# First batch's squares summed on VectorE, wider unread products and a later sigmoid table in a cross-covariance attention and gated feed-forward kernel

## The chip, the cores and the metric

One core of one Trainium2 chip. The metric is the device time of one launch in microseconds; medians of several launches are given with their range. The runs were spread over four chips, each round with runs of the kernel before of its own. A profile is one more execution with the hardware profiler, and its span (first to last recorded instruction) is some 2 us shorter than the time of the launch.

## The reference, cut to what matters

```
B, N, C = 4, 6016, 256                       # q, k, v; d_ff = 1536
qn = q / (norm(q over N) + 1e-6);  kn likewise
s  = kn^T @ qn / tau                          # C x C per batch
a  = softmax(s)
x  = (v @ a) as 24064 x 256
out = (sigmoid(x @ w_gate) * (x @ w_val)) @ w_out
```

Per batch, everything up to `a` is a reduction over N. So the first batch's q and k have to be in before any token of its output can start; the later batches' reductions run beside the feed-forward of the batch before.

## The kernel before

q and k of batch 0 come in 13 groups: eleven of four 128-row tiles (numbered 0 to 10), one of two tiles, one of one. Per group VectorE squares q, ScalarE squares k, TensorE adds to the scores, and the column sums of the squares are one-column products with a vector of ones. Between these stand products that nobody reads, there to keep the array's clock up (without those of groups 0 to 8, in run b0 below, group 10's scores took 1.87 us instead of 1.03).

```
def norm_mms(ps, sqs, nt, first, last, order=(0, 1)):
    for w in order:
        for u in range(nt):
            for j in range(CB):               # 2 per tile and operand: 16 per group
                mm(ps[:, one column], sq[:, u, 128 columns], ones_bf[:, 0:1], ...)

def busy(n):                                  # unread products, 128 wide
    for _ in range(n):
        mm(ps[:, :P], ones_bf, ones_bf, True, True)

busy(40)
for g, (t0, nt) in enumerate(groups0):
    sq = [squares(q of group) on VectorE, squares(k of group) on ScalarE]
    for u in range(nt): score(0, t0, u)       # 8 products of 256 columns per group
    ...
    if full: busy(6)
    norm_mms(ps_n0, sq, nt, g == 0, g == last0, ...)
    if full and not the last full one: busy(6)
# norms -> ps_rk -> x -> exp -> e, then the products of e with the expert weights:
sums(0, 0)
gh(0, 0, psg, "g", act=False)                 # act: which engine evicts it
gh(0, 1, psv, "v", act=True)
nc.scalar.preload_act_table(ACT.Sigmoid)
sums(0, 1, pss, "s")
gh(0, 2, psg, "g", act=False)
gh(0, 3, psv, "v", act=False)
gh(0, 4, pso, "o", act=True)
# ... (cut) the steady loop: glu(f): gate and val products, sigmoid, multiply;
# in its first seven steps also gh(0, 5 + f, pso, "o")
```

Products 0 to 4 of e with the weights, their evictions (gh_G, gh_H) and the load of the sigmoid table are a serial passage ahead of the loop.

## Time and profile before

| | before |
|---|---|
| median of 6 runs | 832.36 us (832.06 to 832.71) |
| span of the profile | 830.4 us |
| group 10's scores begin (the loads are in) | 32.33 us |
| from there to the first ps_rk product | 3.47 us |
| from ps_rk to the first ps_o product | 20.09 us |
| from the first ps_o to the end | 774.5 us |

These four rows cut the span at TensorE's own events, and they add up to it. The first is set by the loads, the next two are the serial passage and the first loop steps, the last is steady work that the change does not touch. The profile lines are in the prediction.

### The profile page before, as it was taken

The page shows a single profiled execution, that of the slowest core. Times are in us where ns is not written, and L with a number is a line of the kernel's source. Part 1 is how long each engine was busy: PE and PEld are TensorE (multiplying, and loading weights), DVE is VectorE, ACT ScalarE, POOL GpSimd, SP SyncE. Part 2 cuts the span into 40 slices and gives each one's busy share as a digit, 9 for nine tenths or more (in the row PEclk, how much of TensorE's full clock was granted, in tenths as well). Part 3 has the DMA queues.
Part 4 walks back from the last instruction along what each step waited for, and adds up shares of the span by engine and source line. Part 5 has one row for each costly group of instructions (what it writes and reads, how often), then busy time and mean ns, then how long its engine had stood idle before and what let it go on. Part 6 is the DMA issues. An engine that isn't in the chain of part 4 may idle for free.

```text
span 830.4 us, 14273 instructions
## 1 busy us (share of the span) xinstructions
PE 818.9 (99%) x5463; PEld 513.8 (62%) x5474; DVE 570.4 (69%) x981; ACT 390.8 (47%) x642; POOL 82.9 (10%) x159
## 2 busy tenths in 40 slices
PE   8899999999999999999999999999999999999998
PEld 7656666666666666665576666666566566666666
DVE  2477777777667777777767777777766666666664
ACT  4554444445644444444654444444555444444442
POOL 5532100002110100000220020000000000000000
PEclk9999999999999999999999999999999999999999
DMA  9999623236755543233974453223222324323211
GB/s 209 207 206 189 130 52 88 51 63 123 141 105 105 102 105 60 56 52 79 161 140 97 84 112 77 51 75 66 62 56 65 75 51 82 71 49 69 47 36 71
DMA packets 78740, 77.21 MB, mean 93 GB/s; under 512 B 50768, under 2 KB 55632, under 8 KB 78672
## 3 DMA queue, kind: packets, MB, share of 16 engines
q0 software_dynamic: 23920, 38.81, 28.2%
q1 hardware_dynamic: 54608, 36.97, 17.4%
q8 instruction: 43, 0.70, 0.3%
q10 hardware_dynamic: 144, 0.52, 0.2%
q14 instruction: 25, 0.20, 0.1%
HBM read 78.64 MB, written 24.64 MB: 124 GB/s over the span
## 4 chain that ended last, share of the span: by engine, by line
PE 95%; DMA 3%; DVE 1%; issue 0%; POOL 0%; ACT 0%; POOLq 0%; DVEq 0%; ACTq 0%
PE ps_o L88 30%; PE ps_gate L88 29%; PE ps_val L88 29%; PE ps_s L88 4%; DMA k_sb<-in_k_dram 3%; PE ps_gh L88 2%; PE ps_n L88 0%; DVE gh_G L363 0%; PE ps_busy L88 0%; POOL q_sb L97 0%; PE ps_r L88 0%; DVE hT L408 0%; PE ps_rk L88 0%; DVE gh_H L363 0%; DVE x_sb L293 0%
## 5 line engine op out<-in xcount | busy, mean ns | idle before, releaser
L408 DVE TENSOR_TENSOR hT<-ps_val,g_sb 128x512 bf16<-128x512 f32 (+1 forms) x576 | 391.4, 680 | 214.7 <-ACT g_sb L407 209.5
L407 ACT ACTIVATE g_sb<-ps_gate 128x512 bf16<-128x512 f32 (+1 forms) x576 | 338.2, 588 | 386.6 <-PE ps_gate L88 379.0
L88 PE MATMUL ps_gate<-vT,gh_G 128*128 128x512 bf16 (+1 forms) x1152 | 337.6, 375 | 0.6 <-ACT g_sb L407 0.4
L88 PE MATMUL ps_val<-vT,gh_H 128*128 128x512 bf16 (+1 forms) x1152 | 337.7, 375 | 0.2
L88 PE MATMUL ps_o<-w_out_sb,hT 128*128 128x256 bf16 x2256 | 326.2, 273 | 0.0
L88 PEld LDWEIGHTS <-hT 128*128 128x128 bf16 x2256 | 220.7, 98 | 124.7
L88 PEld LDWEIGHTS <-gh_H 128*128 128x128 bf16 x1152 | 112.7, 98 | 131.5 <-DVE gh_H L363 0.5
L88 PEld LDWEIGHTS <-gh_G 128*128 128x128 bf16 x1152 | 112.5, 98 | 37.9 <-issue 0.6
L106 POOL DMA_DIRECT2D v_sb<-in_v_dram x48 | 25.6, 533 | 625.6 <-DMA vT<-v_sb 517.4
L434 DVE COPY out_sb<-ps_o 128x256 f32<-128x256 f32 x188 | 77.8, 414 | 13.5 <-PE ps_o L88 13.5
L88 PE MATMUL ps_s<-k_sb,q_sb 128*128 128x256 bf16 x376 | 66.8, 275 | 4.9 <-DMA k_sb<-in_k_dram 3.2
L212 DVE TENSOR_TENSOR acc<-acc,sq 128x1024 bf16<-128x1024 bf16 (+1 forms) x66 | 44.2, 670 | 0.0
L88 PEld LDWEIGHTS <-q_sb 128*128 128x128 bf16 x376 | 36.8, 98 | 11.1 <-issue 4.5
L173 DVE TENSOR_TENSOR sq<-q_sb 128x1024 bf16<-128x1024 bf16 (+2 forms) x45 | 30.0, 669 | 18.5 <-DMA q_sb<-in_q_dram 10.7
L97 POOL DMA_DIRECT2D q_sb<-in_q_dram x48 | 26.3, 548 | 15.6 <-DMA q_sb<-in_q_dram 7.9
L97 POOL DMA_DIRECT2D k_sb<-in_k_dram x48 | 26.4, 550 | 12.0 <-ACT g_sb L407 5.4
L173 DVE TENSOR_TENSOR sq<-k_sb 128x1024 bf16<-128x1024 bf16 (+2 forms) x34 | 22.4, 658 | 1.1 <-PE ps_n L88 1.1
L361 ACT ACTIVATE gh_G<-ps_gh,rrow 128x512 bf16<-128x512 f32 x22 | 15.1, 687 | 12.9 <-PE ps_gh L88 9.1
L171 ACT ACTIVATE sq<-k_sb 128x1024 bf16<-128x1024 bf16 (+1 forms) x12 | 12.1, 1020 | 14.7 <-DMA k_sb<-in_k_dram 13.2
L363 DVE TENSOR_SCALAR gh_H<-ps_gh,rrow 128x512 bf16<-128x512 f32 x23 | 17.1, 743 | 1.6 <-PE ps_gh L88 1.6
L88 PE MATMUL ps_busy<-ones_bf 128*128 128x128 bf16 x182 | 16.6, 244 | 1.1 <-DVE shift L125 1.1
L88 PEld LDWEIGHTS <-ones_bf 128*128 128x128 bf16 x194 | 14.6, 110 | 1.5 <-DVE shift L125 1.1
(54 smaller groups left out, 112.6 us busy)
## 6 DMA issues: line engine op xcount, KB each, us to landing
out_dram<-out_sb SPq DMA_DIRECT2D x44, 512.0 KB, 2.9
v_sb<-in_v_dram POOLq DMA_DIRECT2D x44, 256.0 KB, 3.9
q_sb<-in_q_dram POOLq DMA_DIRECT2D x43, 256.0 KB, 7.1
k_sb<-in_k_dram POOLq DMA_DIRECT2D x43, 256.0 KB, 8.3
out_dram<-out_sb SPq DMA_DIRECT2D x4, 384.0 KB, 2.5
w_gate<-in_moe_w_gate_dram POOLq DMA_DIRECT2D x3, 256.0 KB, 6.8
w_val<-in_moe_w_val_dram POOLq DMA_DIRECT2D x3, 256.0 KB, 6.8
w_out_sb<-in_moe_w_out_dram POOLq DMA_DIRECT2D x1, 768.0 KB, 11.9
```

Of the source, the lines that this page charges most:

```text
L88: nc.tensor.matmul(out, lhsT=lhsT, rhs=rhs, start=start, stop=stop, **kw)
L97: nc.gpsimd.dma_start(out=tl[:, :nt, :], in_=rows(src, b)[:, t0 : t0 + nt, :])
L106: nc.gpsimd.dma_start(out=v_sb[:, :nt, :], in_=rows(v, b)[:, t0 : t0 + nt, :])
L171: nc.scalar.activation(out=sq[:, :nt, :], in_=src[:, :nt, :], func=ACT.Square)
L173: engine.tensor_tensor(out=sq[:, :nt, :], in0=src[:, :nt, :], in1=src[:, :nt, :], op=ALU.mult)
L212: nc.vector.tensor_tensor(out=acc[:, :nt, :], in0=acc[:, :nt, :], in1=st[b]["sq", w][:, :nt, :], op=ALU.add)
L361: nc.scalar.activation(out=dst, in_=ps, func=ACT.Copy, scale=r)
L363: nc.vector.tensor_scalar(out=dst, in0=ps, scalar1=r, scalar2=None, op0=ALU.mult)
L407: nc.scalar.activation(out=g_sb[:, :n], in_=ps_gate[:, :n], func=ACT.Sigmoid)
L408: nc.vector.tensor_tensor(out=hts[b, ci][:, f, :n], in0=ps_val[:, :n], in1=g_sb[:, :n], op=ALU.mult)
L434: nc.vector.tensor_copy(out=out_sb[:, s, :], in_=ps)
```

## The change

Its intent: the one-column products of groups 0 to 8 give way to sums on VectorE, which waits for data there; fewer and wider unread products; and product 3 is evicted by ScalarE before it loads the sigmoid table, product 4 by VectorE.

```diff
-            mm(ps[:, :P], ones_bf, ones_bf, True, True)
-    busy(40)
+            mm(ps, ones_bf, ones_wide, True, True)      # 512 wide
+    busy(9)
+    n_acc = NT // TPC - 2                               # 9
     for g, (t0, nt) in enumerate(groups0):
+        if 0 < g < n_acc:
+            for w in range(2):
+                nc.vector.tensor_tensor(out=acc[w], in0=acc[w], in1=sq[w], op=ALU.add)
         for u in range(nt):
             score(0, t0, u)
-        ... busy(6), norm_mms(sq of every group), busy(6)
+        if g < n_acc:
+            busy(5)
+        elif g == n_acc:
+            norm_mms(ps_n0, acc, TPC, True, False)
+            norm_mms(ps_n0, sq, nt, False, False)
+        elif nt == TPC:
+            busy(2)
+            norm_mms(ps_n0, sq, nt, False, False)
         ... (the last two groups as before)
-    busy(12) ... busy(4)
+    busy(3) ... busy(1)
     gh(0, 1, psv, "v", act=True)
-    nc.scalar.preload_act_table(ACT.Sigmoid)
     sums(0, 1, pss, "s")
     gh(0, 2, psg, "g", act=False)
-    gh(0, 3, psv, "v", act=False)
-    gh(0, 4, pso, "o", act=True)
+    gh(0, 3, psv, "v", act=True)
+    nc.scalar.preload_act_table(ACT.Sigmoid)
+    gh(0, 4, pso, "o", act=False)
```

More of the change, by code (lines that the diff above doesn't have):

```diff
@@ L123 @@
     nc.vector.memset(ones_bf, 1.0)
+    ones_wide = consts.tile([P, CH], BF16)
+    nc.vector.memset(ones_wide, 1.0)
     shift = consts.tile([P, 1], FP32)
@@ L153, in score @@
         if t0 == 0 and u == 0:
-            st[b] = {"s": pss.tile([P, CB, C], FP32, tag="s", name="ps_s")}
+            st.setdefault(b, {})["s"] = pss.tile([P, CB, C], FP32, tag="s", name="ps_s")
         ps_s = st[b]["s"]
@@ L165, in score, with squares @@
             )
-    def squares(b, t0, nt, which, engine):
+    def squares(b, t0, nt, which, engine, sq=None):
         src = qk[b, t0][which]
-        sq = sqpool.tile([P, TPC, C], BF16, tag=f"sq{which}", name=f"sq{which}")
+        if sq is None:
+            sq = sqpool.tile([P, TPC, C], BF16, tag=f"sq{which}", name=f"sq{which}")
         if engine is nc.scalar:
@@ L193, in acc_start @@
     def acc_start(b):
-        st[b]["acc"] = [
+        st.setdefault(b, {})["acc"] = [
             attp.tile([P, TPC, C], BF16, tag=f"acc{w}", name=f"acc{w}") for w in range(2)
@@ L442, in busy @@
         for _ in range(n):
-            mm(ps[:, :P], ones_bf, ones_bf, True, True)
-    busy(40)
+            mm(ps, ones_bf, ones_wide, True, True)
+    busy(9)
     ps_n0 = psm.tile([P, 2 * CB], FP32, tag="m", name="ps_n")
+    n_acc = NT // TPC - 2
+    acc_start(0)
+    acc = st[0]["acc"]
     last0 = len(groups0) - 1
     for g, (t0, nt) in enumerate(groups0):
-        full = nt == TPC
         engines = (nc.vector, nc.scalar) if g < last0 else (nc.scalar, nc.vector)
-        sq = [squares(0, t0, nt, w, engines[w]) for w in range(2)]
+        sq = [squares(0, t0, nt, w, engines[w], acc[w] if g == 0 else None) for w in range(2)]
+        if 0 < g < n_acc:
+            for w in range(2):
+                nc.vector.tensor_tensor(out=acc[w], in0=acc[w], in1=sq[w], op=ALU.add)
         for u in range(nt):
             score(0, t0, u)
-        if g == last0:
-            norm_mms(ps_n0, *held, False, False)
-        if full:
-            busy(6)
-        if g == last0 - 1:
+        if g < n_acc:
[6 more added lines that the diff above has]
+            norm_mms(ps_n0, sq, nt, False, False)
+        elif g < last0:
             held = (sq, nt)
         else:
-            norm_mms(ps_n0, sq, nt, g == 0, g == last0, (0, 1) if g < last0 else (1, 0))
-        if full and t0 + nt < head:
-            busy(6)
+            norm_mms(ps_n0, *held, False, False)
+            norm_mms(ps_n0, sq, nt, False, True, (1, 0))
     st[0]["n"] = ps_n0
@@ L469 @@
     copy_s(0, 1)
-    busy(12)
+    busy(3)
     spread_k(0)
-    busy(4)
+    busy(1)
     scale_k(0, 0)
```

## The prediction

In the paragraph before "The change part by part", "the load" of 1.28 us is that of the sigmoid table. "Cold" means the time of a product there: 111 ns each for the opening ones against 56 ns later.

> **What bounds the kernel now.** I read the page first, for the bound of the whole span, then the chain of waits and the timeline of the first 60 us, because the change touches only what lies ahead of the long steady part.
>
> ```profile
> PE 818.9 (99%) x5463; PEld 513.8 (62%) x5474; DVE 570.4 (69%) x981; ACT 390.8 (47%) x642; POOL 82.9 (10%) x159
> ...
> PE 95%; DMA 3%; DVE 1%; issue 0%; POOL 0%; ACT 0%; POOLq 0%; DVEq 0%; ACTq 0%
> ```
>
> The first line is busy time, the second the engines' shares of the chain that ended last. TensorE carries 95% of the span of 830.4 us, VectorE 1%. The 3% of DMA is 27.7 us at the start. There the chain of waits reads (start, length, what):
>
> ```profile
> 11.10 10.43 DMA k_sb<-in_k_dram
> 21.52 0.28 issue
> 21.80 10.48 DMA k_sb<-in_k_dram
> 32.28 0.04 issue
> 32.33 1.03 PE ps_s L88 x8
> 33.36 0.34 PE ps_busy L88 x6
> 33.70 0.38 PE ps_n L88 x16
> ```
>
> Until 32.28 us the end is set by the first batch's q and k coming in; the stretches of that window show the queues full, at 204 to 210 GB/s. A group of q and k is 2 x 256 KB, 0.524 MB, so at 209 GB/s one lands every 2.5 us; the scores of successive groups do start at 24.14, 26.59 and 29.13 us. What TensorE does with one group is in the timeline:
>
> ```profile
> 26.59 1.03 PE L88 MATMUL ps_s<-k_sb,q_sb 128*128 128x256 bf16 x8 [0.34 <-DMA k_sb<-in_k_dram]
> 27.46 0.50 PE L88 MATMUL ps_busy<-ones_bf 128*128 128x128 bf16 x6
> 27.79 0.54 PE L88 MATMUL ps_n<-ones_bf,sq 128*128 128x1 bf16 x16
> 28.20 0.49 PE L88 MATMUL ps_busy<-ones_bf 128*128 128x128 bf16 x6
> 29.13 1.03 PE L88 MATMUL ps_s<-k_sb,q_sb 128*128 128x256 bf16 x8 [0.44 <-DMA k_sb<-in_k_dram]
> ```
>
> The bracket is idle time ahead of the row and what ended it: TensorE has some 0.5 us to spare in each group of 2.5 us. So nothing that shortens its work there can show. From 32.33 to 41.02 us a serial passage follows (last scores, norms, exp, the first products of e with the expert weights and their evictions), and from 41.02 us TensorE is back to back to the end. **Only the passage from 32.28 to about 44 us can move the time.**
>
> [...] the 40 first unread products take 4.45 us, 111 ns each (cold, N=128); later six of them take 0.34 us of the chain, 56 ns each, and two 512-wide ones 0.43 us, 216 ns each. [...] No wait before exceeds 1.7 us, and no group after 10.3 us runs cold. [...] In the trace the q issues on GpSimd that overlap a squaring on VectorE (at 12.35 us, 0.16 us into one) take 0.53 us, as do the k issues that overlap none. [...] The load takes 1.28 us here; [...] the load begins at 39.55, as the eviction before it ends (38.85 + 0.69 = 39.54), and the next operation starts at 40.85. I use 1.28.
>
> **The change part by part.**
>
> (a) Squares summed on VectorE. Groups 0 to 8 lose 9 x 16 = 144 one-column products and gain 16 on the sums: 128 fewer, about 128 x 24 ns (0.38 us for 16 in the chain) = 3.1 us of TensorE, all of it in the DMA-bound stretch: worth nothing. VectorE gains 8 x 2 = 16 additions of 128x1024 bf16, by the steady loop's row:
>
> ```profile
> L212 DVE TENSOR_TENSOR acc<-acc,sq 128x1024 bf16<-128x1024 bf16 (+1 forms) x66 | 44.2, 670 | 0.0
> ```
>
> 16 x 0.67 = 10.7 us. Per group VectorE then has 0.69 (q's square) + 2 x 0.67 = 2.03 us, under the 2.5 us of the transfers. Does the sum come in time? k of group 8 lands at about 26.6; ScalarE squares it by 27.7; the last addition is done by 28.5. TensorE asks for the sums at about 30.0, after group 9's scores. Group 9's q square waits up to 0.5 us more and is still 0.9 us early. Worth 0.
>
> (b) Wider unread products. Per group, five 512-wide ones, 5 x 0.216 = 1.08 us, replace 12 x 0.056 + 16 x 0.024 = 1.06 us, so a warm group stays near 1.95 us. On the path are group 10's: 2 x 0.216 = 0.43 in place of 6 x 0.056 = 0.34, between its scores and its norms: **+0.10 us**. Later, 3 x 0.216 = 0.65 replaces 0.67 and 1 x 0.216 replaces 0.22: 0. [...] TensorE waits for data until 7.17 anyway: 0.
>
> (c) Table and evictions. ScalarE and VectorE now read (both in one timeline; here ACT and DVE rows alone):
>
> ```profile
> 39.55 1.28 ACT L486 ACT_TABLE_LOAD   x1
> ...
> 40.22 0.74 DVE L363 TENSOR_SCALAR gh_H<-ps_gh,rrow 128x512 bf16<-128x512 f32 x1
> ...
> 40.85 0.69 ACT L361 ACTIVATE gh_G<-ps_gh,rrow 128x512 bf16<-128x512 f32 x1
> ...
> 41.44 0.59 ACT L407 ACTIVATE g_sb<-ps_gate 128x512 bf16<-128x512 f32 x1
> ...
> 42.06 0.69 DVE L408 TENSOR_TENSOR hT<-ps_val,g_sb 128x512 bf16<-128x512 f32 x1 [1.10 <-ACT g_sb L407]
> ```
>
> The chain runs through gh_H (40.22 to 40.97) into ps_val at 41.02. After: that eviction goes to ScalarE, its product ready at 39.72, so 39.77 to 40.46. The second ps_val product then waits only for TensorE's order: second gate product 40.37, then 40.58, 40.80. **-0.23 us.** But the table load moves to 40.47 to 41.75, and the first sigmoid from 41.44 to about 41.76: 0.32 later. Behind it VectorE multiplies (to 43.06 instead of 42.75) and then evicts product 5, ending near 43.71 instead of 43.40. Product 7 reuses that PSUM buffer (two rotate). It began at 43.83; with 0.23 gained TensorE wants it at 43.60 but gets it at about 43.75. **Given back: about 0.15 us.** After this each loop step is 1.29 us on TensorE against at most 0.69 + 0.74/2 = 1.06 on VectorE and 0.59 + 0.69/2 = 0.94 on ScalarE, so the lag drains.
>
> **Sum:** +0.10 - 0.23 + 0.15 = +0.02 us, an estimate good to perhaps 0.3. From about 44 us on the instructions of every engine are as before. The one later stall, 0.36 us of TensorE waiting for a sigmoid at 52.6 us, hangs on TensorE's own order and shifts with it. So 832.23 + 0.02, say **832.2 us**.
>
> **The rivals.**
>
> 1. *A new wait on VectorE at the start.* If additions ran slower or pushed back GpSimd's issues, the q and k loads would starve. For: VectorE nearly doubles its work (0.69 to 2.03 us of 2.5). Against: a load takes 10.4 us from issue to landing, four groups queued ahead, so a delay of 0.7 us is swallowed. If wrong, +0.3 to +1 us: 5%.
>
> 2. *The clock falls back.* In group 9 nothing wide follows the scores any more: 32 one-column products, then idle from about 30.8 to 32.33 us, 1.5 us against 1.1 before. [...] TensorE could run at half clock through the passage; it has some 3 us of work between 32.3 and 37 us, so +1 to +3 us. Against: [...] before, 0.45 to 1.7 us of idle did no harm. 8%.
>
> 3. *The table move is worth more.* If the 0.32 us lag of the sigmoid never reaches product 7, the full 0.23 us stays, and with product spacing in its favour the gain is 0.3 us or so: 832.0 us. 30%.
>
> 4. *The lag is worth more.* If sigmoid and eviction queue on ScalarE for several steps, the two gate buffers run out and TensorE loses 0.2 to 0.5 us: 832.6 us. 25%.
>
> 5. *TensorE gets its 3.1 us back.* It would need TensorE to be the bound before 32 us; the idle brackets speak against it. 2%.
>
> **Range and chances.** The three runs before spread 0.56 us (832.15 to 832.71), rivals 3 and 4 span -0.3 to +0.5 us around the centre, rival 2 adds a thin tail upwards. 8 in 10: 831.5 to 833.0 us. A change of 2% is 16.6 us, more than half of all the time ahead of the steady part; no part of this change reaches that: 0.99 within.
>
> **What would show it.** In the profile after: group 10's scores still begin at 32.3 us (within 0.2) with a DMA wait ahead, and the q and k transfers still take some 10.4 us; 16 additions of 0.67 us on VectorE, the last before 28.7 us; unread products 0.216 us apart after about 10.5 us; about 0.1 us more between group 10's scores and its norms; gh_H of the fourth product on ScalarE, the second load right behind it, the first sigmoid near 41.8 us; product 7 waiting briefly for VectorE; TensorE in the same place by 56 us (first ps_o at 55.9 within 0.3). The prediction is wrong if the first loads end at another time, if matmuls after 32 us take double, or if the shift at the first ps_o is not the shift of the end.

## The result

831.76 us (median of 6 runs, 831.52 to 832.92) against 832.36 us: ratio 0.9994, 95% interval 0.9982 to 1.0007. (A ratio is the mean time of one kernel's runs over that of the other's of the same rounds, so it is not quite the ratio of the medians.) The size is as predicted, 0.6 us or 0.07% off the old median. The profile shows that it does not come from where the prediction looked.

The page of the changed kernel, busy times and the engines' shares of the chain that ended last:

```profile
PE 816.5 (98%) x5210; PEld 503.4 (61%) x5224; DVE 580.9 (70%) x998; ACT 391.0 (47%) x642; POOL 83.2 (10%) x159
...
PE 95%; DMA 3%; issue 0%; POOL 0%; DVE 0%; ACT 0%; POOLq 0%; ACTq 0%
```

VectorE's share of the chain fell from 1% to 0%, TensorE has 503 instructions fewer (matmuls and weight loads), and the bound is the same. The chain of waits of the changed kernel about the end of the loads (start, length, what):

```profile
10.93 9.74 DMA k_sb<-in_k_dram
20.66 0.28 issue
20.95 10.70 DMA k_sb<-in_k_dram
31.64 0.04 issue
31.69 1.03 PE ps_s L88 x8
32.72 0.22 PE ps_busy L88
32.94 0.05 issue
32.99 0.54 PE ps_n L88 x16
```

Set beside the same lines of before: the two loads on the chain take 20.4 us together instead of 20.9, and group 10's scores begin 0.64 us earlier. By the four rows:

| | before | after | difference |
|---|---|---|---|
| group 10's scores begin | 32.33 | 31.69 | -0.64 |
| to ps_rk | 3.47 | 3.57 | +0.10 |
| to the first ps_o | 20.09 | 20.04 | -0.05 |
| to the end | 774.5 | 774.5 | 0.0 |

The passage, on which the prediction spent its working, is +0.05 us all told (+0.02 predicted). The 0.64 us are in the loads, which the change was held not to touch. In the changed kernel's timeline the loads have one hitch:

```profile
23.29 1.03 PE L88 MATMUL ps_s<-k_sb,q_sb 128*128 128x256 bf16 x8 [0.47 <-DMA k_sb<-in_k_dram]
24.16 1.24 PE L88 MATMUL ps_busy<-ones_wide,ones_bf 128*128 128x512 bf16 x4
26.74 1.03 PE L88 MATMUL ps_s<-k_sb,q_sb 128*128 128x256 bf16 x8 [1.33 <-DMA k_sb<-in_k_dram]
```

From group 7 to group 8 it is 3.45 us instead of 2.5. Looking at the DMA queues microsecond by microsecond for what lies there, one finds this in the stretch from 24 to 25 us (queue, packets, MB, share of 16 engines; the shares add up to more than 100%, so packets overlap in time on an engine):

```profile
q0 software_dynamic: 110, 0.21, 113.2%
q8 instruction: 1, 0.02, 6.1%
```

One packet of instructions, of 16 KB, took 6.1% of 16 engines' microsecond, which is 0.98 us of one engine, in the midst of the loads. The same view of the kernel before has three of them, starting at 13.5, 21.2 and 30.2 us. Here the third, in the stretch from 30 to 31 us, and group 10's scores from the timeline:

```profile
q0 software_dynamic: 186, 0.19, 112.6%
q8 instruction: 1, 0.02, 5.6%
...
32.33 1.03 PE L88 MATMUL ps_s<-k_sb,q_sb 128*128 128x256 bf16 x8 [1.09 <-DMA k_sb<-in_k_dram]
```

Group 9's scores began at 29.13 us, so the same hitch, 3.20 us instead of 2.5, stood in the profile before, in lines that the prediction shows.

Queue q8, which the profile calls "instruction", has 43 packets before (0.70 MB, some 16 KB each) and 41 after (0.67 MB). TensorE's matmuls and weight loads are 10,937 and 10,434, which is 254 to a packet in both. So I take this for TensorE's instruction stream, which the change shortened where the loads are the bound. TensorE itself worked on through the packet of 24.4 us: its unread products ran from 24.16 to 25.40 us.

### The profile page after: what moved, and what is told of

The parts are those of the page before. It is cut to its first block, busy times and chain, and to the rows that moved or that the text cites. A ratio compares the mean times of both kernels' runs of the same rounds, so it can differ in the third digit from the quotient of the medians.

```text
span 829.8 us, 13778 instructions
## 1 busy us (share of the span) xinstructions
PE 816.5 (98%) x5210; PEld 503.4 (61%) x5224; DVE 580.9 (70%) x998; ACT 391.0 (47%) x642; POOL 83.2 (10%) x159
## 4 chain that ended last, share of the span: by engine, by line
PE 95%; DMA 3%; issue 0%; POOL 0%; DVE 0%; ACT 0%; POOLq 0%; ACTq 0%
PE ps_o L88 30%; PE ps_gate L88 29%; PE ps_val L88 29%; PE ps_s L88 4%; DMA k_sb<-in_k_dram 3%; PE ps_gh L88 2%; PE ps_n L88 0%; POOL q_sb L97 0%; PE ps_busy L88 0%; DVE hT L411 0%; PE ps_rk L88 0%; DVE x_sb L296 0%; ACT g_sb L410 0%; POOL k_sb L97 0%; ACT e_sb L309 0%
## 5 line engine op out<-in xcount | busy, mean ns | idle before, releaser
L437 DVE COPY out_sb<-ps_o 128x256 f32<-128x256 f32 x188 | 77.6, 413 | 13.5 <-PE ps_o L88 13.5
L88 PE MATMUL ps_busy<-ones_wide,ones_bf 128*128 128x512 bf16 x57 | 16.1, 408 | 1.7 <-DVE shift L127 1.6
L460 DVE TENSOR_TENSOR acc<-acc,sq 128x1024 bf16<-128x1024 bf16 x16 | 11.1, 692 | 5.7 <-ACT sq L174 5.4
```

What stands on the lines that cost most here:

```text
L88: nc.tensor.matmul(out, lhsT=lhsT, rhs=rhs, start=start, stop=stop, **kw)
L437: nc.vector.tensor_copy(out=out_sb[:, s, :], in_=ps)
L460: nc.vector.tensor_tensor(out=acc[w], in0=acc[w], in1=sq[w], op=ALU.add)
```

## The experiments

**Two theories.** (A) The loads come in earlier because fewer instruction packets get in their way. (B) The 0.64 us are chance of the loads, or the work of VectorE or the idleness of TensorE. The first four runs were made to measure chance and to split the change, before the packets had been found.

**1. Both kernels again**, unchanged.

> The kernel before, unchanged, for the scatter of the arrival of the first loads. Theory (the 0.64 us by which group 10's scores began earlier in the changed kernel, 31.69 against 32.33 us, is chance of the loads): the scores of group 10 begin anywhere from 31.5 to 32.6 us here too, and the passage from there to the first ps_o is 23.56 us within 0.1 (32.33 to 55.89 in the first profile). Rival (the change brings the loads in earlier): again 32.3 us within 0.2. Time: ratio 1.000.

> The changed kernel, unchanged, with more rounds. Theory of chance: group 10's scores begin anywhere from 31.5 to 32.6 us, the passage to the first ps_o is 23.61 us within 0.1 (31.69 to 55.30), ratio 0.9990 to 1.0005. Rival (loads earlier by the change): 31.7 us again within 0.2, ratio 0.9993 and clear of 1.

**2. Parts alone.** The first has the change but this, the second is the kernel before plus it:

```diff
 # a1_sums_wide_only (against the changed kernel); c1_evictions_only is its reverse on the kernel before
-    gh(0, 3, psv, "v", act=True)
-    nc.scalar.preload_act_table(ACT.Sigmoid)    # after product 3
-    gh(0, 4, pso, "o", act=False)
+    nc.scalar.preload_act_table(ACT.Sigmoid)    # after product 1
+    gh(0, 3, psv, "v", act=False)
+    gh(0, 4, pso, "o", act=True)
```

> Squares summed on VectorE and wider unread products, but table load and evictions as before. Theory: the part from group 10's scores to the ps_rk products is 3.57 us as in the changed kernel (3.47 before), the rest to the first ps_o 20.09 us as before, together 23.66; arrival as chance has it. Rival (the sums bring the loads in earlier): arrival at 31.7 us. Ratio 0.9990 to 1.0005.

> The kernel before with only the table load and the evictions of the change. Theory: group 10's scores to ps_rk 3.47 us, from ps_rk to the first ps_o 20.04 us (20.09 before), together 23.51; the first sigmoid 0.3 us later and product 7 waiting for VectorE. Rival (the move is worth its whole 0.23 us): 19.86 us from ps_rk to the first ps_o. Ratio 0.9990 to 1.0005 either way.

Measured, all against the same nine runs of the kernel before (832.61 us, 831.98 to 832.72):

| run | median us (5 runs) | group 10's scores | to ps_rk | to first ps_o | instruction packets before 31 us |
|---|---|---|---|---|---|
| n0_before_again | 832.16 | 31.88 | 3.47 | 20.09 | 3 |
| c1_evictions_only | 832.50 | 32.22 | 3.47 | 20.04 | 3 |
| n1_after_again | 831.56 | 31.48 | 3.58 | 20.04 | 1 |
| a1_sums_wide_only | 831.63 | 31.88 | 3.58 | 20.09 | 1 |

The passage came out as expected in all four, to 0.02 us, and its parts add: the wide products cost 0.10 us to ps_rk, the evictions save 0.05 us. In c1 the first sigmoid comes 0.32 us later after ps_rk (5.96 us instead of 5.64) and product 7 waits 0.19 us, as expected. The medians settle nothing: n0 is the kernel before, and yet 0.45 us under the nine runs. Nor do the expected arrivals: n0's 31.88 us misses the rival's range, and n1's 31.48 us lies 0.02 us outside both of its ranges, with a ratio of 0.9990 that is not clear of 1 (0.9977 to 1.0002). The arrival scatters by half a microsecond from run to run, partly because the very first transfer does (its scores begin between 6.43 and 7.17 us in my profiles). So part of the first 0.64 us was chance. But the kernels with fewer TensorE instructions are the earlier ones on average: 31.69, 31.48 and 31.88 (mean 31.68) against 32.33, 31.88 and 32.22 (mean 32.14), 0.46 us.

**3. Instruction count apart from TensorE's time.** Three edits of the changed kernel:

```diff
 # x1_many_thin                    # x2_seven_wide         # b0_no_unread
-            busy(5)               -            busy(5)    -            busy(5)
+            busy(2)               +            busy(7)    +            pass
+            thin(32)    # unread, one column
```

> The changed kernel, but in groups 0 to 8 two wide unread products and 32 unread one-column products stand for five wide ones: 29 more matmuls per group, 522 more TensorE instructions in all before group 10, while a group takes TensorE 0.87 + 0.43 + 0.86 = 2.2 us, still under the 2.5 us of the loads. Theory (what the change gained is TensorE's instruction stream, [...]): three instruction packets before 31 us as in the kernel before, instead of one; group 10's scores at 31.9 to 32.3 us, span 830.0 to 830.5 (829.7 for the changed kernel). Rival (chance, or VectorE's sums, which stay): one packet, scores at 31.5 to 31.9 us, span 829.7.

> The changed kernel with seven wide unread products per group instead of five: TensorE works 0.87 + 7 x 0.216 = 2.38 us in a group, as much as or more than with the many thin ones, with only 36 more instructions. Theory of the instruction packets: one packet, at most two, before 31 us; scores at 31.4 to 31.9 us, span 829.7 within 0.2. Rival (it is TensorE's time in a group that holds up the loads): as late as with the thin products, span above 830.0.

> The changed kernel without unread products in groups 0 to 8 (the opening nine stay). Two things: the instruction packet that came at 24.5 us should come only with the norms at about 30.5 us, so the loads should be in 0 to 0.5 us earlier, scores at 31.0 to 31.7 us. And TensorE then works 0.87 us in 2.5: if the clock falls to half, a group's scores take 1.7 to 1.9 us and the passage from group 10's scores to the first ps_o, 23.61 us before, grows by 1 to 3 us; if the unread products buy nothing, it stays at 23.6 within 0.1.

The packets came as foretold: three, one and none before 31 us; the 522 instructions that x1 has more brought two packets more. To take the chance of the first transfer out, I measure the loads by ScalarE's squares of k, from the start of group 0's to the start of group 10's, in every profile:

| packets before 31 us | kernels | group 0 to group 10, us |
|---|---|---|
| none | b0_no_unread, v2_late_warm (below) | 24.15, 23.97 |
| one | changed kernel twice, a1, x2, and e5, v1, b10 (below) | 24.92, 24.80, 24.87, 25.09, 24.94, 25.11, 24.82 |
| two | w1 (below) | 25.08 |
| three | kernel before twice, c1, x1 | 25.23, 25.02, 25.41, 25.18 |

The first two rows are far apart: means of 24.06 and 24.94 us. The last, with a mean of 25.21, overlaps the second at its edge (25.02 against 25.11). **In the mean the first packet costs the loads some 0.9 us, the second and third together some 0.3 us more.** The same squares, taken from group to group, show where the time goes, because the one packet falls at another time in each of these kernels:

| kernel | packet starts at | group 6 to 7 | 7 to 8 | 8 to 9 | 9 to 10 |
|---|---|---|---|---|---|
| v2_late_warm | none | 2.57 | 2.45 | 2.56 | 2.45 |
| b0_no_unread | none | 2.56 | 2.45 | 2.56 | 2.46 |
| b10_ten_wide | 20.4 | **3.39** | 2.47 | 2.55 | 2.47 |
| x2_seven_wide | 22.0 | **3.67** | 2.48 | 2.53 | 2.47 |
| changed kernel | 24.4 | 2.59 | **3.44** | 2.48 | 2.47 |
| v1_few_instructions | 26.9 | 2.53 | 2.48 | **3.64** | 2.51 |

One interval in each row is longer by 0.8 to 1.1 us, the one in which the packet falls; no other differs from the rows without a packet by more than 0.08 us. ScalarE's rows of v1 about it:

```profile
25.77 1.06 ACT L174 ACTIVATE sq<-k_sb 128x1024 bf16<-128x1024 bf16 x1 [1.43 <-DMA k_sb<-in_k_dram]
29.41 1.06 ACT L174 ACTIVATE sq<-k_sb 128x1024 bf16<-128x1024 bf16 x1 [2.58 <-DMA k_sb<-in_k_dram]
```

Theory B fails here. It is not TensorE's idleness that brings the loads in early in b0 and v2: with TensorE at work without a pause (b10, x2) the groups away from the packet come at the same pace. And VectorE works alike in x1, x2, b0 and the changed kernel, whose loads take 25.18, 25.09, 24.15 and 24.92 us.

Not every packet costs as much. Of the three in the kernel before (twice), c1 and x1, the first makes its interval 0.68 to 0.95 us longer, the second 0.01 to 0.15, the third 0.05 to 0.75; in w1 the two cost 0.67 and 0.65, and the last interval gives 0.44 back. Why is open. At 209 GB/s over 16 engines 16 KB are some 1.25 us of one engine's work (an estimate from these three figures), so a group that had to wait for its slowest engine would be held up by about what is measured; but the trace does not tell which engine took a packet, so this is argued and not shown.

In absolute arrival I missed: x1 came at 31.64 us (31.9 to 32.3 expected), since its first transfer was early, and x2 at 31.95, just over its range, TensorE being used up in every group: its scores start 2.38 us apart without a wait. The span of x2's profile, 830.1 us, is outside its range too (829.7 within 0.2) and is the one that the rival foretold; its other four runs have 829.6 to 829.8. b0 came at 30.52, earlier than I had dared to say.

x1 and b0 show a second thing, the clock. Group 10 in x1's timeline, and group 10 in b0's:

```profile
29.82 0.54 PE L88 MATMUL ps_n<-ones_bf,acc 128*128 128x1 bf16 x16
30.23 0.54 PE L88 MATMUL ps_n<-ones_bf,sq 128*128 128x1 bf16 x16
31.64 1.76 PE L88 MATMUL ps_s<-k_sb,q_sb 128*128 128x256 bf16 x8 [0.87 <-DMA k_sb<-in_k_dram]
```

```profile
28.06 1.03 PE L88 MATMUL ps_s<-k_sb,q_sb 128*128 128x256 bf16 x8 [0.87 <-DMA k_sb<-in_k_dram]
...
30.52 1.87 PE L88 MATMUL ps_s<-k_sb,q_sb 128*128 128x256 bf16 x8 [0.64 <-DMA k_sb<-in_k_dram]
```

The same eight products take 1.03 us at full and 1.76 to 1.87 at half clock. That it is half, the two wide products behind them show: 0.86 us in x1 and 0.85 in b0 up to the norms, 0.43 in the changed kernel. (The mean granted clock of the profiled run is 0.997 in x1, 0.989 in b0 and 1.0 in the changed kernel.) From group 10's scores to ps_rk it is then 5.05 and 4.96 us instead of 3.57. In b0 that gives back what the early loads gained: 832.01 us (831.82 to 832.29), no faster. In x1 three of five runs had a span of 831.1 to 831.3 us and two of 829.6 and 829.7, median 833.01 us; the profiled one was of the long sort and cold. The two short ones are as short as the changed kernel's, so the cost of two more packets does not show in them; two runs are too few to tell. The changed kernel has one long run in its first six, 832.92 us with a span of 831.0 and a mean clock of 0.998 (0.999 or 1 in the others, though the kernel before has 0.998 in runs that are not long). It was not profiled; that it fell cold in group 9, where it too has only one-column products, is likely but not shown. x2: 831.69 us (831.57 to 832.03).

**4. Where TensorE's spare time ends.** `busy(5)` becomes `busy(10)`.

> The changed kernel with ten wide unread products per group: 0.87 + 2.16 = 3.03 us of TensorE per group. Theory (0.5 us to spare in a group of 2.5 us): TensorE becomes the bound of the first stretch, its DMA waits before the scores vanish, and group 10's scores begin near 6.8 + 9 x 3.03 + 1.7 = 35.8 us, the time 4 us longer. Rival (the loads set the end whatever TensorE does): 31.5 to 32 us.

Scores at 35.80 us, time 835.87 us (one run). The working of TensorE's share of a group is right to 0.1 us, so the gain of the change is not TensorE's time: that was to spare. The loads themselves came no later than in the changed kernel (24.82 against 24.92 us).

**5. The wide products alone**, on the kernel before:

```diff
-            mm(ps[:, :P], ones_bf, ones_bf, True, True)     # busy(40); 6 + 6 per group; 12; 4
+            mm(ps, ones_bf, ones_wide, True, True)          # busy(9);  2 + 3 per group;  3; 1
```

> The kernel before with only the wider unread products (9 at the start, 2 and 3 in a group, 3 and 1 later); the norms stay one-column products. 540 TensorE instructions by the end of group 9 instead of some 800: two instruction packets before 31 us instead of three. [...] the arrival is between the two kernels, group 10's scores at 31.5 to 32.2 us. A second thing: in the kernels with the sums and wide products the measured time exceeds the span by 1.9 to 2.0 us, in those without by 2.3; if the wide products bring it, this kernel has 1.95, if the sums do, 2.3.

Two packets (15.3 and 27.4 us), scores at 31.86 us, 832.03 us (831.71 to 832.07) against 832.62 of its rounds. The second expectation held as well: the time exceeds the span by 1.93 to 2.01 us here, as in every kernel with the wide tile (1.89 to 2.01), while it is 2.25 to 2.42 us in the kernel before and in c1. So some 0.36 us of the gain lies outside the recorded span and comes with the wide products or their tile of ones, not with VectorE's sums. It does not hang on the opening products (v1 and v2 below have none and show 1.91 to 1.99) nor, it seems, on the length of the instruction stream (x1's is as long as before). What it is stays open.

**6. Two attempts on the passage and the packets.** The first issues product 5 ahead of the first gate product; the second does that too and thins out TensorE's instructions.

```diff
 # e5_early_product                                 # v1_few_instructions: as e5, and
     gh(0, 4, pso, "o", act=False)                  -    busy(9)
+    gh(0, 5, pso, "o", act=False)                  -    n_acc = NT // TPC - 2
 ...                                                +    n_acc = NT // TPC - 1
-                    gh(0, 5 + f, pso, "o")         -            busy(5)
+                    gh(0, 6 + f, pso, "o")         +            busy(3)
```

> The changed kernel with product 5 of e and the expert weights issued before the first gate products and evicted by VectorE ahead of its first multiplication. Theory (the gain of the table move, 0.23 us, was given back by product 7 waiting for VectorE's late eviction of product 5, and TensorE has a hole ahead of the second gate product): from ps_rk to the first ps_o 19.7 us within 0.1 instead of 20.04. Rival (the loop hides it anyway): 20.0 us.

> The early product 5, and as few TensorE instructions ahead of group 10 as the clock may allow: no opening unread products, three wide ones per group in groups 0 to 9, group 9 summed on VectorE as well, the norms of the sums after group 10's scores. Theory (the first instruction packet costs the loads about 1 us): no packet before 30 us, group 10's scores at 30.5 to 31.0 us, 3.54 us to ps_rk, 19.7 to the first ps_o, span 828.3 to 828.9, time 830.3 to 830.9. Rival (the early arrival without unread products came from TensorE's idleness, not from the packet): scores at 31.5 us or later. If the clock falls back, the part from the scores to ps_rk is 4.9 us instead of 3.54.

e5 took 20.28 us from ps_rk to ps_o, not 19.7. Its chain of waits says why:

```profile
32.67 7.46 DMA w_val<-in_moe_w_val_dram
40.13 0.04 issue
40.17 0.59 PE ps_gh L88 x2
```

Product 5 needs the second slice of w_val, which landed only at 40.13 us; moved forward, it found TensorE waiting 0.53 us for it. 832.00 us (831.81 to 832.73). In v1 a packet still came, at 26.9 us, so scores at 31.88 us tell nothing of a missing packet, though its groups up to there kept the pace of the kernels without one (table above). Its 3.54 us to ps_rk are as worked out; from there to ps_o it took 20.21 us, not 19.7; and 831.95 us (831.65 to 832.09) is no gain.

**7. Unread products only in groups 7 to 9.**

```diff
-    busy(9)
-    n_acc = NT // TPC - 2
+    n_acc = NT // TPC - 1
-            busy(5)
+            busy(5 if g >= 7 else 0)
```

> The changed kernel with the unread products only where the clock matters: none at the start, none in groups 0 to 6, five wide ones in each of groups 7, 8 and 9, group 9 summed on VectorE too and the norms of the sums after group 10's scores. Some 190 TensorE instructions by 30.5 us, fewer than the 242 of the run without unread products, in which no packet came before 31 us. Theory (the first packet costs about 1 us, and only the clock took that gain back there): no packet before 30 us, group 10's scores at 30.5 to 31.0 us, 3.54 us from there to ps_rk as in the run with few instructions, 20.04 to the first ps_o, span 828.5 to 829.1, time 830.4 to 831.0. Rival (a lightly used array brings the loads in early, not the missing packet): scores at 31.5 us or later, span 829.6 or more. If the clock is cold at group 10: 4.9 us to ps_rk.

No packet before 32 us, and the loads were the quickest of all (23.97 us). ScalarE squared group 10's k at 30.98 us. These are its rows in the timeline, with the idle time ahead and what ended it in the bracket (VectorE's square of q, named in the second, ended at 30.91 us; in b0, where the pace is the same, the transfer is named):

```profile
28.53 1.06 ACT L174 ACTIVATE sq<-k_sb 128x1024 bf16<-128x1024 bf16 x1 [1.51 <-DMA k_sb<-in_k_dram]
30.98 1.06 ACT L174 ACTIVATE sq<-k_sb 128x1024 bf16<-128x1024 bf16 x1 [1.39 <-DVE sq L176]
```

But TensorE reached group 10 only at 31.65 us, without a wait for data before it. After waits of 1.41 to 1.54 us ahead of the scores of groups 3 to 5 it had been at half clock from group 5's scores, below, into group 8's, which took 1.50 us at 27.27 us (group 4's and group 9's took 1.03 and 1.04; the mean granted clock of the run is 0.994):

```profile
18.47 1.87 PE L88 MATMUL ps_s<-k_sb,q_sb 128*128 128x256 bf16 x8 [1.54 <-DMA k_sb<-in_k_dram]
```

Group 7's scores and unread products took 3.8 us (1.95 for a group of the changed kernel, 6.83 to 8.78 us), and two groups later TensorE had not caught up. From group 10's scores to ps_rk it took 3.54 us, as expected: the clock was back. 832.05 us (831.39 to 832.76), the same. The expectation of 830.4 to 831.0 us was wrong, for this reason: the loads gained what theory A says, and warming the array too late spent it. No kernel has a median under the changed one's (831.56 us in n1).

## Why the prediction was right or wrong

The time (832.2 predicted, 831.76 measured) and "within 2%" were right. By its steps:

- **What bounds the kernel**: right. TensorE can spare some 0.5 us per group: run b10 confirms it to 0.1 us.
- **(a) Squares on VectorE "worth nothing"**: the argument about TensorE's and VectorE's time was right; 16 additions appeared, each 0.69 us (0.67 taken), the last done at 28.56 us. The step that failed is "So nothing that shortens its work there can show". It counted TensorE's time and not TensorE's instructions, whose packets go among the loads that were the bound; where only one does, it holds a group up by 0.8 to 1.1 us. Fewer instructions left one packet of 16 KB instead of three: 0.46 us of arrival in the mean of three profiles each, 0.36 us by the intervals from group 0 to group 10 (25.22 against 24.86). This counts (a) and (b) together; (b) alone, w1, leaves two packets.
- **(b) Wider products +0.10 us**: measured +0.10 (3.47 to 3.57 or 3.58) in the changed kernel's profiles and in a1's. The nine opening products took 3.50 us, the 40 before 4.45, and TensorE then waited 1.73 us for data (1.67 before): 0, as foretold. Not foreseen: the 0.36 us outside the span.
- **(c) Table and evictions, -0.23 and +0.15**: the mechanism came out as written. The timeline of the changed kernel (ACT, DVE and PE rows):

```profile
39.22 0.69 ACT L364 ACTIVATE gh_H<-ps_gh,rrow 128x512 bf16<-128x512 f32 x1 [0.23 <-PE ps_gh L88]
...
39.93 1.28 ACT L501 ACT_TABLE_LOAD   x1
...
41.22 1.09 ACT L410 ACTIVATE g_sb<-ps_gate 128x512 bf16<-128x512 f32 x2
...
41.85 0.69 DVE L411 TENSOR_TENSOR hT<-ps_val,g_sb 128x512 bf16<-128x512 f32 x1 [1.43 <-ACT g_sb L410]
...
42.46 0.74 DVE L366 TENSOR_SCALAR gh_H<-ps_gh,rrow 128x512 bf16<-128x512 f32 x1
...
43.25 0.59 PE L88 MATMUL ps_gh<-w_val,e_sb 128*128 128x512 bf16 x2
```

  gh_H is evicted with the load right behind it; the second ps_val product comes 5.00 us after ps_rk instead of 5.22 (-0.22). Product 7 (last line) waits from 43.06, when the products before it are through, to 43.25 for VectorE's eviction of product 5 (42.46 to 43.20): 0.19 us given back. Net -0.04 at product 7 and -0.05 at the first ps_o, where -0.08 was foretold.
- **Rivals.** Rival 2, the clock, was rated 8% and is real in its surroundings: x1, with less wide work in the groups before but the same group 9 as the changed kernel, falls to half clock at group 10 (its scores take 1.76 us instead of 1.03), and it costs 1.5 us. That 0.45 to 1.7 us of idle had done no harm before was no safe ground: in x1 the hole from the end of group 9's wide work to group 10 was 1.8 us, filled in part by one-column products, and in v2 waits of 1.41 to 1.54 us came ahead of the slow scores. Rivals 3 and 4 did not come true; rival 1 did not show (the loads still took about 10 us, with VectorE fuller). Rival 5 was rightly put aside; TensorE got no time back.
- **"The prediction is wrong if the first loads end at another time"**: by its own test of 0.2 us, group 10's scores at 31.69 against 32.3 us were outside, and so was the first ps_o, at 55.30 against 55.9 us within 0.3. That the total held is luck: a gain of 0.60 us that the account did not have just fitted into a range of 0.75 us to each side.
- **Smaller slips of its working.** VectorE's work per group nearly triples (0.69 to 2.03 us), it does not "nearly double". 16.6 us is 40% of the 41.02 us ahead of the steady loop, not "more than half". And "one lands every 2.5 us" passes over the last group of its own trace (3.20 us).

How the medians add up: loads -0.36 by the intervals (-0.46 by the arrival, the chance of the first transfer included), passage +0.05, outside the span -0.36, together -0.67 to -0.77 us; measured -0.60 in the first comparison and -1.05 in the second. These two intervals, like those of all other ratios, include no change at all. At this size the cuts of the profile decide, not the medians.

## What to carry to other kernels

Where transfers are the bound, count the instructions of the busiest engine too: here a 16 KB packet came for some 254 of them, in the midst of the loads, and one such packet held up a group by up to 1.1 us. Filler made of few wide operations needs fewer of them than filler made of many narrow ones (five for twelve in a group here). When a part is said to be free because its engine waits anyway, ask what else it uses. And cut the span at a few events of the bounding engine before comparing kernels: 0.1 us in 830 could be told so, where no comparison of medians was clear of no change.
